# Rebuilding the sequence passes of a spectral-plus-GEGLU kernel: panels in pairs, other queues for late operands and stores, and the last down products in the passes' own banks

## The chip, the cores and the metric

The kernel runs on one core of one Trainium2 chip. The metric is the device time of one execution, in microseconds. Before the change three runs took 846.03, 844.85 and 843.11 us, median 844.85.

## The reference

The kernel computes a block with two parallel branches that are added to their input. x is 2048 tokens by 512 features, the inner size of the second branch is 1792.

```python
x = A_x
xn = _layernorm(x, axis=-1)
# branch A: Fourier mixing, DFT along the features, then along the sequence, real part
a = jnp.einsum("bsd,ed->bse", xn, dft_hid_re)
b = jnp.einsum("bsd,ed->bse", xn, dft_hid_im)
A = jnp.einsum("ts,bse->bte", dft_seq_re, a) - jnp.einsum("ts,bse->bte", dft_seq_im, b)
# branch B: GEGLU
B = jnp.einsum("bsf,fd->bsd", _gelu(xn @ w_gate) * (xn @ w_up), w_down)
return x + A + B
```

All values are float32. The sums of the sequence DFT run over 2048 tokens.

## The kernel before, in words

**Arithmetic.** A float32 product is made from three matmuls. Each operand is split into a high part, which ACT copies into the reduced type (`split_hi`, L72), and a low part, which DVE gets by subtraction (`split_lo`, L75). `mm3` (L84 to L87) adds high by high and the two crossed terms in one PSUM bank. Products of two-by-two blocks are made with seven products (numbered 0 to 6) instead of eight, on sums of blocks; what the seven products mean for the four output blocks is settled by sums before and after.

**Stages.** Up to 53 us: layernorm and the first part of the feature DFT. Then 14 units of gate and up products, in which the down products (`down`, L441) run as background items; a second part of the feature DFT; 14 more units up to 485.7 us. From there to 836.4 us run the sequence passes, with the last 14 down items among them; the change is nearly all here.

**The sequence passes.** `steps` is a list of four passes of 16 steps; a step is one block of 128 tokens that is summed over. `passes` is (0,0), (1,0), (0,1), (1,1): the column c of the output and the group g. Group 0 makes products 0, 6 and 2 (18 matmuls a step, for two row blocks j), group 1 products 5, 4, 3 and 1 (24 matmuls). A product keeps two PSUM banks through a pass. All eight banks are one pool. For a step:

- `load_step` (L639) loads the panels of the sequence DFT matrix, 128x512 each (256 KB), three for group 0 and four for group 1, on SP's queue; `sum_step` (L646) adds panels on DVE; `split_step` (L659) makes high and low parts of each.
- The other operand, the "side", comes from the scratch tensors `ab` and `sd` in DRAM. In the first pass `load_side` (L688, SP's queue) and `side_split` (L694) prepare what group 0 needs, and it stays in memory. What group 1 needs, `b` and `qr` of each token, is the late side: `load_late` (L701) issues the two loads on POOL's queue two steps ahead and `late_side` (L707) splits them; 12 tokens are done in the second pass and 4 in the third (`late_at`).
- `contract` (L777) issues the matmuls.

At the end of a pass `drain` (L738) empties the banks and `seed` (L728) fills them for the next pass, by an ACT copy of what `load_acc` (L722) has read from the scratch tensor `partial`, where the down products and the input's own terms have been added up. The drains of group 0 send adding transfers on POOL's queue (a DMA that adds to what lies in DRAM): `tot` to `partial` (L747) and `neg` to the output (L754). Those of group 1 send `v` to the output the same way (L762) and store the finished blocks with `store` (L734) on SP's queue.

**What sets the order.** The program is written out by hand, and each engine and each queue takes its instructions in the order written. The loop over `steps` (from L917) prepares panels ahead: a step's loads are issued four or fewer steps ahead (`split_upto`), its sums one step before its splits. An issue on a queue waits for the tile that it writes to be free, and what stands behind waits with it.

Of the kernel before, what the change touches and what calls it, by code (L numbers as in the profile page):

```python
# [14 lines left out]
P = 128  # L15
# [20 lines left out]
def fnet_geglu_kernel(ctx: ExitStack, tc: tile.TileContext, x, xt, cs, dh, wgu, wd, out):  # L36
# [64 lines left out]
    xnt = dram.tile([2, ND, P, CH], F32, name="xnt")  # L101

# [336 lines left out]
    D_ORDER = (0, 2, 1, 5, 4, 6, 3)  # L439
# [20 lines left out]
    def more_items(q):  # L460
        i = q % (NP // 2)
        if i == 0:
            items.extend([lambda r=r: down([q], r, range(2)) for r in D_ORDER])
        elif i % 2 == 0:
            items.extend([lambda r=r, j=j: down([q - 1, q], r, [j]) for r in D_ORDER for j in range(2)])

# [6 lines left out]
    def background(n):  # L473
# [21 lines left out]
        if n % 2 == 0 and n:  # L495
            for k in range(4):
                splits(h_split, n // 2 - 1, k)
# [24 lines left out]
    def unit(n):  # L522
# [9 lines left out]
        if n == 1:  # L532
            store_stats()
        if n in (3, 7):
            load_st((n - 3) // 4)
# [39 lines left out]
        if n == 2 * NP - 1:  # L575
            for r in SEEDED[0]:
                load_acc(0, r)
# [23 lines left out]
        if n == 2 * NP - 1:  # L601
            seed(0, SEEDED[0][0])
# [5 lines left out]
        if n == 2 * NP - 1:  # L608
            seed(0, SEEDED[0][1])
# [11 lines left out]
    SEEDED = {0: (2, 6), 1: (5, 4, 3, 1)}  # L621
    passes = [(0, 0), (1, 0), (0, 1), (1, 1)]
    steps = [(c, g, n) for c, g in passes for n in range(NS)]
    pan, pan_src, pan_hl = {}, {}, {}
# [7 lines left out]
    def split_upto(i):  # L632
        return max(i + 1, min(i + 2, 2 * NS)) if i > 2 else i + 1

    def order(i):
        c, g, n = steps[i]
        return GROUP[g] if n else SEEDED[g] + GROUP[g][:1 - g]

    def load_step(i):  # L639
        if i < len(steps):  # L640
            c, g, n = steps[i]
            for m, t in ((0, 0), (0, 1), (1, 1), (1, 0))[:3 + g]:
                pan[i, m, t] = slot("pan")
                nc.sync.dma_start(pan[i, m, t], cs[2 * c + t, m, n])

    def sum_step(i):  # L646
        if i < len(steps):
            g = steps[i][1]
            c0, c1, i1, i0 = (pan.pop((i, m, t), None) for m, t in ((0, 0), (0, 1), (1, 1), (1, 0)))
            if g == 0:  # L650
                nc.vector.tensor_add(c1, c1, i1)
                pan_src[i] = {0: c0, 6: c1, 2: i1}
            else:
                nc.vector.tensor_add(c0, c0, c1)
                nc.vector.tensor_add(c1, c0, i1)
                nc.vector.tensor_add(i1, c1, i0)
                pan_src[i] = {4: c0, 5: c1, 3: i1, 1: i0}

    def split_step(i, part=slice(None)):  # L659
        if i < len(steps):  # L660
            src = pan_src[i]
            for r in order(i)[part]:
                t = pair("ps") if i < 4 else None
                pan_hl[i, r] = (t[:, 0], t[:, 1]) if i < 4 else hl_tile("ps")
                split(pan_hl[i, r], src[r])

    av, bv, qr, w34, a0, s34, b_hl, qr_hl = ({} for _ in range(8))
# [19 lines left out]

    def load_side(n):  # L688
        if n < NS:
            av[n], w34[n] = slot("ar", F32, (P, HD)), slot("w34")  # L690
            nc.sync.dma_start(av[n], ab[n, 0, :, :HD])
            nc.sync.dma_start(w34[n], sd[n, 0])

    def side_split(n):  # L694
        if n < NS:
            t = pair("s34")
            a0[n], s34[n] = hl_half("a0"), (t[:, 0], t[:, 1])
            split(a0[n], av.pop(n))
            split(s34[n], w34.pop(n))

    def load_late(n):  # L701
        if n < NS:
            bv[n], qr[n] = slot("b"), slot("qr")
            nc.gpsimd.dma_start(bv[n], ab[n, 1])
            nc.gpsimd.dma_start(qr[n], sd[n, 1])

    def late_side(n):  # L707
        b_hl[n], t = hl_tile("bt"), pair("qrhl")
        qr_hl[n] = t[:, 0], t[:, 1]
        split(b_hl[n], bv.pop(n))  # L710
        split(qr_hl[n], qr.pop(n))
# [8 lines left out]
    acc, bank = {}, {}  # L720

    def load_acc(c, r):  # L722
        t = pair("acc", F32)
        for j in range(2):
            acc[c, r, j] = t[:, j]
            nc.gpsimd.dma_start(acc[c, r, j], partial[c, r, j])

    def seed(c, r):  # L728
        for j in range(2):
            bank[c, r, j] = ps_tile("m")  # L730
            nc.scalar.activation(bank[c, r, j], acc.pop((c, r, j)), AF.Copy)  # L731

    def store(c, h, j, src):
        nc.sync.dma_start(out[2 * h + j, 2 * c], src)  # L734

    us, vs = {}, {}

    def drain(c, r, j):  # L738
        ps = bank.pop((c, r, j))
        if r in (0, 6):  # L740
            t = ship("tot")
            if r == 0:
                nc.vector.tensor_add(t, ps, acc.pop((c, r, j)))
            else:
                nc.scalar.activation(t, ps, AF.Copy)
            for u in (5, 1) if r == 0 else (3,):
                nc.gpsimd.dma_start(partial[c, u, j], t, accum_op=OP.add)  # L747
        if r in (6, 2):
            t = ship("neg")
            if r == 6:  # L750
                nc.vector.tensor_scalar_mul(t, ps, -1.0)
            else:
                nc.scalar.activation(t, ps, AF.Copy, scale=-1.0)
            nc.gpsimd.dma_start(out[2 * int(r == 6) + j, 2 * c + 1], t, accum_op=OP.add)  # L754
        if r == 5:
            us[j] = ship("u")
            nc.scalar.activation(us[j], ps, AF.Copy)
        if r == 4:
# [4 lines left out]
        if r == 3:  # L763
            nc.vector.tensor_add(us[j], ps, us[j])
            store(c, 1, j, us[j])
        if r == 1:
# [239 lines left out]
```

## Time and profile before

| | us |
|---|---|
| median of three runs | 844.85 |
| profiled execution | 845.09 |
| its span, first to last instruction | 843.3 |
| sequence passes in it, TensorE's first to last matmul | 485.69 to 836.38 |
| TensorE busy | 808.4 |
| VectorE (DVE) busy | 690.6 |
| ScalarE (ACT) busy | 505.9 |
| GpSimd (POOL) busy | 197.6 |
| mean granted TensorE clock | 0.986 of full |

The profile is one execution taken by the hardware profiler. PE is TensorE's matmuls, PEld its weight loads, which run beside them; SP, ACT and POOL also issue DMAs, and SPq or POOLq is the waiting of a queue's issue for a semaphore. A group of instructions is named by its source line, engine and operation, `out<-in` with the program's names, the shapes, and the count; behind the bar stand its busy time, the mean of one in ns, and the idle time of the engine before it with what ended that. The chain that ended last is followed back from the last instruction: at each step to what released it. "m" are the banks of the passes, "dn" those of down products, "psh" and "psl" the high and low parts of panels.

### The profile page before, as it was taken

The page shows a single profiled execution, that of the slowest core. Times are in us where ns is not written, and L with a number is a line of the kernel's source. Part 1 is how long each engine was busy: PE and PEld are TensorE (multiplying, and loading weights), DVE is VectorE, ACT ScalarE, POOL GpSimd, SP SyncE. Part 2 cuts the span into 40 slices and gives each one's busy share as a digit, 9 for nine tenths or more (in the row PEclk, how much of TensorE's full clock was granted, in tenths as well). Part 3 has the DMA queues.
Part 4 walks back from the last instruction along what each step waited for, and adds up shares of the span by engine and source line. Part 5 has one row for each costly group of instructions (what it writes and reads, how often), then busy time and mean ns, then how long its engine had stood idle before and what let it go on. Part 6 is the DMA issues. An engine that isn't in the chain of part 4 may idle for free.

```text
span 843.3 us, 11706 instructions
## 1 busy us (share of the span) xinstructions
PE 808.4 (96%) x3514; PEld 657.0 (78%) x3514; DVE 690.6 (82%) x1288; ACT 505.9 (60%) x972; POOL 197.6 (23%) x294
## 2 busy tenths in 40 slices
PE   8999999999999999999999999998798789999996
PEld 4887878888878888888888878886586568877885
DVE  6778999888999589998898898772896699769971
ACT  5666875767777467676756867661766254465531
POOL 2410222222211333342322401233442320010001
PEclk9999999999999999999999999999799979999999
DMA  9933638787953598899789898999889976688714
GB/s 344 377 103 125 200 103 185 166 184 164 213 162 127 173 243 214 243 265 210 178 189 270 230 282 236 317 343 282 299 322 334 278 240 212 188 233 258 245 57 99
DMA packets 92543, 187.44 MB, mean 222 GB/s; under 512 B 11568, under 2 KB 14144, under 8 KB 92224
## 3 DMA queue, kind: packets, MB, share of 16 engines
q1 hardware_dynamic: 62240, 110.92, 39.5%
q0 software_dynamic: 29952, 75.52, 37.3%
q8 instruction: 27, 0.44, 0.2%
q14 instruction: 36, 0.29, 0.1%
q10 hardware_dynamic: 288, 0.26, 0.1%
HBM read 128.97 MB, written 61.87 MB: 226 GB/s over the span
## 4 chain that ended last, share of the span: by engine, by line
PE 80%; DVE 6%; DMA 5%; issue 4%; POOL 2%; ACT 2%; SPq 0%; DVEq 0%; POOLq 0%; ACTq 0%
PE m L86 30%; PE dn L86 14%; PE b L86 11%; PE a L86 8%; PE c L86 8%; PE xp L86 5%; PE sb L86 2%; DMA pan<-in_cs 2%; DMA b<-ab 2%; PE sa L86 1%; POOL partial L747 1%; DMA xraw<-xnt 1%; DVE ws L369 1%; DMA acc<-partial 1%; POOL out_y L754 1%
## 5 line engine op out<-in xcount | busy, mean ns | idle before, releaser
L72 ACT ACTIVATE psh<-pan 128x512 fp32r<-128x512 f32 x212 | 120.7, 622 | 99.5 <-PE m L86 57.3
L75 DVE TENSOR_TENSOR psl<-pan,psh 128x512 fp32r<-128x512 f32 x212 | 134.3, 684 | 17.4 <-ACT psh L72 14.0
L455 POOL DMA_DIRECT2D partial<-part x92 | 80.8, 891 | 194.1 <-ACT part L451 177.1
L86 PE MATMUL m<-psh,qrhl 128*128 128x512 f32 x256 | 86.2, 398 | 5.4 <-ACT psh L72 4.4
L451 ACT ACTIVATE part<-dn 128x512 f32<-128x512 f32 x112 | 65.8, 598 | 23.1 <-PE dn L86 21.2
L86 PE MATMUL m<-psh,s 128*128 128x512 f32 x224 | 74.3, 394 | 0.0
L86 PEld LDWEIGHTS m<-psh,qrhl 128*128 128x128 f32 x256 | 49.1, 192 | 16.4 <-ACT psh L72 4.8
L86 PE MATMUL m<-psl,qrhl 128*128 128x512 f32 x128 | 51.3, 401 | 7.1 <-DVE psl L75 7.1
L75 DVE TENSOR_TENSOR wl<-ws,wh 128x512 fp32r<-128x512 f32 x84 | 55.0, 684 | 0.0
L86 PE MATMUL m<-psh,bth 128*128 128x512 f32 x128 | 50.1, 392 | 1.3 <-ACT m L731 1.3
L72 ACT ACTIVATE wh<-ws 128x512 fp32r<-128x512 f32 x84 | 49.6, 629 | 2.1 <-PE dn L86 2.1
L86 PE MATMUL m<-psh,btl 128*128 128x512 f32 x128 | 49.8, 389 | 0.0
L86 PE MATMUL m<-psl,bth 128*128 128x512 f32 x128 | 49.8, 389 | 0.0
L86 PEld LDWEIGHTS m<-psh,s 128*128 128x128 f32 x224 | 42.8, 191 | 9.0
L86 PE MATMUL m<-psh,a 128*128 128x512 f32 x112 | 40.0, 399 | 8.1 <-ACT psh L72 8.1
L86 PE MATMUL m<-psl,s 128*128 128x512 f32 x112 | 44.1, 393 | 0.0
L762 POOL DMA_DIRECT2D out_y<-v x8 | 7.1, 1089 | 148.0 <-DVE v L82 145.0
L86 PE MATMUL b<-xT3h,w 128*128 128x512 f32 x112 | 39.2, 391 | 0.3 <-ACT w L588 0.3
L591 DVE TENSOR_TENSOR w<-c,w 128x512 f32<-128x512 f32 x28 | 19.3, 690 | 24.4 <-ACT w L588 24.3
L75 DVE TENSOR_TENSOR htl<-s,hth 128x512 fp32r<-128x512 f32 x56 | 35.9, 685 | 2.9 <-ACT hth L72 2.8
L430 DVE TENSOR_TENSOR s<-s 128x512 f32<-128x512 f32 x56 | 37.3, 687 | 0.9
L588 ACT ACTIVATE w<-b 128x512 f32<-128x512 f32 x28 | 16.7, 597 | 35.2 <-PE b L86 35.2
(290 smaller groups left out, 2282.2 us busy)
## 6 DMA issues: line engine op xcount, KB each, us to landing
pan<-in_cs SPq DMA_DIRECT2D x224, 256.0 KB, 4.7
partial<-part POOLq DMA_DIRECT2D x112, 256.0 KB, 5.2
wx<-in_wgu SPq DMA_DIRECT2D x56, 256.0 KB, 4.6
abr<-ab SPq DMA_DIRECT2D x32, 256.0 KB, 6.4
wd<-in_wd SPq DMA_DIRECT2D x28, 256.0 KB, 4.4
acc<-partial POOLq DMA_DIRECT2D x28, 256.0 KB, 5.8
d<-in_dh SPq DMA_DIRECT2D x16, 256.0 KB, 5.4
ab<-ab POOLq DMA_DIRECT2D x16, 256.0 KB, 4.4
```

The lines of the kernel that those rows point to most:

```text
L72: nc.scalar.activation(t[0], src, AF.Copy)
L75: nc.vector.tensor_sub(t[1], src, t[0].bitcast(F32))
L86: nc.tensor.matmul(ps, a[u][:, sl], b[v], start=first and r == 0, stop=last and r == 2, skip_group_check=resumed)
L369: nc.vector.tensor_tensor(r[k][:, h], u, v, op=op)
L430: nc.vector.tensor_sub(t, u, v)
L451: nc.scalar.activation(t, ps[j], AF.Copy)
L455: nc.gpsimd.dma_start(partial[sp, r, j], t, accum_op=OP.add)
L588: nc.scalar.activation(w, b, AF.Copy)
L591: nc.vector.tensor_add(w, c, w)
L747: nc.gpsimd.dma_start(partial[c, u, j], t, accum_op=OP.add)
L754: nc.gpsimd.dma_start(out[2 * int(r == 6) + j, 2 * c + 1], t, accum_op=OP.add)
L762: nc.gpsimd.dma_start(out[2 * h + j, 2 * c + 1], v, accum_op=OP.add)
```

## The change

- **Panels in pairs.** The host lays the DFT matrix out so that one transfer brings two panels, 128x1024 (L645, L646): a step is two transfers, 512 KB + 256 KB in group 0 and two of 512 KB in group 1. The splits of a pair are one ACT and one DVE instruction of 128x1024 (`split_begin`). The bytes stay.
- **Order.** The passes are now (1,0), (0,0), (1,1), (0,1), and the token order in group 1 follows the order in which late sides become ready. Late sides are loaded on SP's queue (L736, L737) two steps ahead: 12 tokens in steps 17 to 28, and the last four at steps 3, 5, 7 and 9 of the third pass and again of the fourth, so that these are made twice.
- **Fewer adding transfers.** `drain` in group 0 writes two results per row block plainly to a new scratch tensor `kept` (L797); product 2 is first subtracted from `xt` on DVE (L822). The adding transfers to the output, eight of `neg` and eight of `v`, are gone, and with them the eight copies of `xt` into the output near the start. In the group-1 passes `load_rest` (L765) reads `kept` and `xt` back, `sub_rest` and `drain_rest` (L808) subtract on DVE, and plain stores follow. The twelve adding transfers of `tot` stay (L819). All stores but the very last go to POOL's queue (L800).
- **Last down products.** For products 0, 6 and 2 the last down products are added by TensorE into the banks of the first pass (`direct`); their ACT copies and adding transfers are gone. All banks of a pass but the first pass's product 2 are now seeded.

The core of the diff:

```diff
+    kept = dram.tile([2, 2, 2, P, CH], F32, name="kept")
...
+        elif q == NP - 1:
+            for r in (0, 2, 1, 6, 5, 4, 3):
+                items.extend([lambda r=r: direct([q - 1, q], r)] if r in GROUP[0] else
+                             [lambda r=r, j=j: down([q - 1, q], r, [j]) for j in range(2)])
...
-    passes = [(0, 0), (1, 0), (0, 1), (1, 1)]
+    passes = [(1, 0), (0, 0), (1, 1), (0, 1)]
+    tokens = {0: list(range(NS)), 1: [0, 1, 2, 3, 4, 12, 5, 13, 6, 14, 7, 15, 8, 9, 10, 11]}
...
-            for m, t in ((0, 0), (0, 1), (1, 1), (1, 0))[:3 + g]:
-                pan[i, m, t] = slot("pan")
-                nc.sync.dma_start(pan[i, m, t], cs[2 * c + t, m, n])
+            a, b = pair("pan", F32), pair("pan", F32) if g else slot("pan1")
+            pan[i] = a, b
+            nc.sync.dma_start(flat(a), cs[c, n, 0])
+            nc.sync.dma_start(flat(b) if g else b, cs[c, n, 1] if g else cs[c, n, 1, :, :CH])
...
     def load_late(n):
-        if n < NS:
-            bv[n], qr[n] = slot("b"), slot("qr")
-            nc.gpsimd.dma_start(bv[n], ab[n, 1])
-            nc.gpsimd.dma_start(qr[n], sd[n, 1])
+        av[n], bv[n] = slot("qr"), slot("b")
+        nc.sync.dma_start(bv[n], ab[n, 1])
+        nc.sync.dma_start(av[n], sd[n, 1])
...
+    def load_rest(c):
+        for j in range(2):
+            rest[c, 0, j], rest[c, 1, j], rest[c, 2, j] = ship("x12"), ship("x22"), slot("kept")
+            for h, src in enumerate((kept[c, 1, j], xt[c, 1, 2 + j], kept[c, 0, j])):
+                nc.gpsimd.dma_start(rest[c, h, j], src)
...
-    def store(c, h, j, src):
-        nc.sync.dma_start(out[2 * h + j, 2 * c], src)
+    def store(c, h, t, j, src):
+        nc.gpsimd.dma_start(out[2 * h + j, 2 * c + t], src)
...
+    def drain_rest(c):
+        for j in range(2):
+            for h in range(2):
+                t = rest.pop((c, h, j))
+                nc.vector.tensor_sub(t, t, vs[j])
+                store(c, h, 1, j, t)
...
         if r in (0, 6):
             t = ship("tot")
-            if r == 0:
-                nc.vector.tensor_add(t, ps, acc.pop((c, r, j)))
-            else:
-                nc.scalar.activation(t, ps, AF.Copy)
+            nc.scalar.activation(t, ps, AF.Copy)
+            if r == 6:
+                keep(c, 0, j, t)
             for u in (5, 1) if r == 0 else (3,):
                 nc.gpsimd.dma_start(partial[c, u, j], t, accum_op=OP.add)
-        if r in (6, 2):
-            t = ship("neg")
...
-            nc.gpsimd.dma_start(out[2 * int(r == 6) + j, 2 * c + 1], t, accum_op=OP.add)
...
+        elif r == 2:
+            t = ship("x2")
+            nc.vector.tensor_sub(t, rest.pop((c, j)), ps)
+            keep(c, 1, j, t)
...
-            v = ship("v")
-            neg_sub(v, ps, us[j])
-            for h in range(2):
-                nc.gpsimd.dma_start(out[2 * h + j, 2 * c + 1], v, accum_op=OP.add)
+            vs[j] = slot("v")
+            nc.vector.tensor_add(vs[j], ps, us[j])
...
+    def direct(qs, r):
+        for j in range(2):
+            for q in qs:
+                mm3(bank[passes[0][0], r, j], wl[("d", q), r], cols(j), hl[q, r], False, False, resumed=r != 2, late=1)
...
-                nc.gpsimd.dma_start(out[2 * h + j, 2 * sp + 1], xt[sp, 1, 2 * h + j])
...
-    late_at = {NS + 2 + k: k for k in range(NS - 4)}
-    late_at.update({2 * NS + 2 * k: NS - 4 + k for k in range(4)})
+    late_at = {NS + 1 + k: n for k, n in enumerate((4, 5, 6, 7, 8, 9, 10, 11, 0, 1, 2, 3))}
+    late_at.update({p * NS + 3 + 2 * k: 12 + k for p in (2, 3) for k in range(4)})
...
-        advance(load_step, ahead + 2)
+        advance(load_step, i + 4)
...
+        if at == 0 and p == 3:
+            drain_rest(passes[2][0])
```

How the order changes on the two queues. POOL's queue at the end of the first pass, before: the ten adding transfers of the drains and the first late loads (`tot` and `neg` are the drained sums, `b` and `qr` the late side).

```order
L747 DMA partial_83<-tot_6292 128x512 x2
L747 DMA partial_83<-tot_6299 128x512 x2
L747 DMA partial_83<-tot_6322 128x512
L754 DMA out_y<-neg_6325 128x512
L747 DMA partial_83<-tot_6331 128x512
L754 DMA out_y<-neg_6334 128x512
L754 DMA out_y<-neg_6341 128x512
L754 DMA out_y<-neg_6347 128x512
L704 DMA b_6356<-ab_84 128x512
L705 DMA qr_6357<-sd_85 128x512
```

The same place after: `x2` is product 2 subtracted from `xt`, and `x12` and `old` are loads late in the second pass.

```order
L819 DMA partial_83<-tot_6190 128x512 x2
L819 DMA partial_83<-tot_6197 128x512 x2
L797 DMA kept_87<-tot_6208 128x512
L819 DMA partial_83<-tot_6208 128x512
L797 DMA kept_87<-tot_6215 128x512
L819 DMA partial_83<-tot_6215 128x512
L797 DMA kept_87<-x2_6226 128x512
L797 DMA kept_87<-x2_6232 128x512
L783 DMA x12_6711<-in_xt 128x512
L783 DMA x12_6713<-in_xt 128x512
```

Six adding transfers and four plain ones are left, and the late loads are no longer behind them. SP's queue at the same place, before: only panels, three to a step.

```order
L644 DMA pan_6350<-in_cs 128x512
L644 DMA pan_6352<-in_cs 128x512
L644 DMA pan_6354<-in_cs 128x512
L644 DMA pan_6393<-in_cs 128x512
L644 DMA pan_6395<-in_cs 128x512
L644 DMA pan_6397<-in_cs 128x512
```

SP's queue there after, from the loads that are issued in the last step of the first pass on:

```order
L646 DMA pan1_6176<-in_cs 128x512
L736 DMA b_6180<-ab_84 128x512
L737 DMA qr_6179<-sd_85 128x512
L645 DMA pan_6244<-in_cs 128x1024
L646 DMA pan1_6245<-in_cs 128x512
L736 DMA b_6249<-ab_84 128x512
L737 DMA qr_6248<-sd_85 128x512
L645 DMA pan_6279<-in_cs 128x1024
```

Each step now has a pair, a single panel and two late operands on this queue. SP's queue at the end of the third pass, before: four stores of finished blocks (`u` and `o`) stand between the panels of the next pass.

```order
L644 DMA pan_7953<-in_cs 128x512
L644 DMA pan_7955<-in_cs 128x512
L734 DMA out_y<-u_7968 128x512
L734 DMA out_y<-u_7973 128x512
L734 DMA out_y<-o_8022 128x512
L734 DMA out_y<-o_8028 128x512
L644 DMA pan_8038<-in_cs 128x512
L644 DMA pan_8040<-in_cs 128x512
```

The same place after:

```order
L645 DMA pan_7592<-in_cs 128x1024
L646 DMA pan_7593<-in_cs 128x1024
L645 DMA pan_7665<-in_cs 128x1024
L646 DMA pan_7666<-in_cs 128x1024
L645 DMA pan_7712<-in_cs 128x1024
L646 DMA pan_7713<-in_cs 128x1024
L736 DMA b_7717<-ab_84 128x512
L737 DMA qr_7716<-sd_85 128x512
```

The stores are gone from this queue; panels follow panels, and the late side of a token that is made a second time comes behind them.

More of the change, by code (lines that the diff above doesn't have):

```diff
@@ L533, in unit @@
             store_stats()
+        if n == 2 * NP - 1:
+            for r in GROUP[0]:
+                load_old(passes[0][0], r)
         if n in (3, 7):
@@ L620, in fnet_geglu_kernel @@
     GROUP = {0: (0, 6, 2), 1: (5, 4, 3, 1)}
-    SEEDED = {0: (2, 6), 1: (5, 4, 3, 1)}
-    passes = [(0, 0), (1, 0), (0, 1), (1, 1)]
-    steps = [(c, g, n) for c, g in passes for n in range(NS)]
-    pan, pan_src, pan_hl = {}, {}, {}
+    passes = [(1, 0), (0, 0), (1, 1), (0, 1)]
+    tokens = {0: list(range(NS)), 1: [0, 1, 2, 3, 4, 12, 5, 13, 6, 14, 7, 15, 8, 9, 10, 11]}
+    steps = [(c, g, n) for c, g in passes for n in tokens[g]]
+    pan, pan_hl = {}, {}
     reached = {}
@@ L630, in advance, with flat @@
         reached[f] = max(upto + 1, reached.get(f, 0))
[L632 to L637, printed above, removed]
+    def flat(t):
+        return t.rearrange("p a b -> p (a b)")
     def load_step(i):
@@ new lines, in sum_step, with prepare_step @@
+    def sum_step(i):
+        for f in sums(i):
+            f()
+    def prepare_step(i):
+        advance(sum_step, i)
+        later = sums(i + 1) if reached[sum_step] == i + 1 else []
+        reached[sum_step] = max(reached[sum_step], i + 2)
+        if reached.get(split_step, 0) <= i < len(steps):
+            reached[split_step] = i + 1
+            low = [split_begin(i, k) for k in range(2)]
+            del pan[i]
+            if len(later) < 2:
+                low[0]()
+                low.pop(0)
+        else:
+            low = []
+        for k in range(max(len(low), len(later))):
+            for f in later[k:k + 1] + low[k:k + 1]:
+                f()
@@ new lines, in split_begin, with split_step @@
+    def split_begin(i, k):
+        g = steps[i][1]
+        two = g or k == 0
+        t = (pair("ps"), pair("pl")) if two else hl_tile("ps1")
+        src = pan[i][k]
+        split_hi(t, src)
+        for h, r in enumerate((((0, 6), (2,)), ((4, 5), (3, 1)))[g][k]):
+            pan_hl[i, r] = [v[:, h] for v in t] if two else t
+        return lambda: split_lo(t, src)
+    def split_step(i):
+        if i < len(steps):
+            for k in range(2):
+                split_begin(i, k)()
+            del pan[i]
@@ L669, in load_ab @@
+    av, bv, a0, s34, b_hl, qr_hl = ({} for _ in range(6))
     def load_ab(n):
@@ L931, in fnet_geglu_kernel @@
[L931 to L942 removed]
+        chores(p, at)
@@ L943, in fnet_geglu_kernel @@
+        ahead = i + 2 if 2 < i < 2 * NS or i > 3 * NS + 4 else i + 1
+        turn = at == NS - 1 and p == 2
+        if turn:
+            split_begin(i + 1, 0)()
+            reached[split_step] = i + 2
+        elif at < NS - 1:
+            for k in range(i + 1, ahead + 1):
+                prepare_step(k)
+        if at == 0 and p == 3:
+            drain_rest(passes[2][0])
         if p == 0:
-            advance(side_split, n + 2)
+            advance(side_split, at + 2)
             while carry:
```

187 lines of the change are left out of this document (96 added, 91 removed).

## The prediction

> **What bounds the kernel now.** I read the page's busy times first, then a table by stretches, then the chain that ended last, then the waits. The first line of the page:
>
> ```profile
> PE 808.4 (96%) x3514; PEld 657.0 (78%) x3514; DVE 690.6 (82%) x1288; ACT 505.9 (60%) x972; POOL 197.6 (23%) x294
> ```
>
> TensorE is the bound over the whole span, but a share of 96% hides places where it stands still. The sequence passes are 485.7 to 836.4 us; this is the table by stretches there (columns: stretch, length, then busy time and count of PE, PEld, DVE, ACT, POOL, then granted clock, DMA share, GB/s):
>
> ```profile
> 485.00:560.00 75.00, 74.86 (x329) 61.21 (x328) 58.80 (x103) 48.55 (x96) 14.75 (x19) 1.00 0.96 289
> 560.00:600.00 40.00, 31.25 (x129) 25.05 (x128) 20.56 (x35) 17.80 (x35) 17.32 (x25) 0.89 1.05 304
> 600.00:644.00 44.00, 44.00 (x193) 36.37 (x192) 40.14 (x67) 27.66 (x51) 12.01 (x22) 0.98 0.92 328
> 644.00:680.00 36.00, 25.34 (x100) 18.75 (x99) 23.38 (x39) 18.07 (x33) 15.61 (x23) 0.90 1.00 272
> 680.00:750.00 70.00, 70.00 (x303) 57.72 (x303) 59.97 (x94) 35.72 (x64) 4.36 (x6) 0.98 0.67 202
> 750.00:765.00 15.00, 11.94 (x53) 9.57 (x52) 11.36 (x19) 6.96 (x14) 0.00 (x0) 1.00 1.04 337
> 765.00:836.00 71.00, 71.00 (x315) 58.75 (x313) 54.84 (x88) 26.62 (x48) 3.51 (x4) 1.00 0.49 145
> ```
>
> Three of seven stretches are holes. The chain that ended last (start, length, what) gives the full pace and names the holes:
>
> ```profile
> 484.96 0.69 DVE ps L75
> 485.69 1.45 PE m L86 x5
> ...
> 499.72 4.08 PE m L86 x18
> 503.80 1.36 PE dn L86 x6
> ...
> 567.59 0.88 POOL partial L747
> ...
> 585.50 0.09 POOL out_y L754
> 586.16 6.87 DMA b<-ab
> 593.12 0.64 ACT bth L72
> 596.33 45.73 PE m L86 x190
> ...
> 645.66 0.56 POOL partial L747
> ...
> 664.88 0.58 POOL out_y L754
> 665.46 7.69 DMA b<-ab
> 678.24 72.46 PE m L86 x308
> 750.70 6.54 DMA pan<-in_cs
> 760.14 76.24 PE m L86 x335
> ```
>
> A step of 18 matmuls takes 4.08 us: 0.2267 us each. The passes hold 576 (two passes of 18 by 16 steps) + 768 (two of 24 by 16) + 84 (the last down products) = 1428 matmuls, 323.7 us at that pace. They take 836.38 − 485.69 = 350.7 us (76.24 us from 760.14 end at 836.38). So **27.0 us are lost**. By the table: 40 − 129 × 0.2267 = 10.8 at the first pass end, 36 − 100 × 0.2267 = 13.3 at the second, 15 − 53 × 0.2267 = 3.0 at the third; these three make the 27.0, and what the other stretches leave over or under is within the records that are missing (about 4 matmuls).
>
> The first two holes read alike. At the pass end POOL issues ten adding transfers in a row, from 567.59 to 585.59 and from 645.66 to 665.46, and only behind them, on the same queue, stands the next late operand `b`. ACT takes its work in order, so it stands at the `b` copy with the next step's panels already in memory:
>
> ```profile
> ACT bth L72 <- DMA b<-ab: 32.1, 2, 19.8
> ...
> SPq L734 <- DVE u L764: 37.8, 4, 30.0
> ```
>
> The third hole is the last line: the stores of the outputs wait on SP's queue for their sums, and the panel loads of the next pass stand behind them; 750.70 is a panel that landed too late.
>
> **The change, part by part.** The sum is made against the profiled execution, 845.09 us with a span of 843.3; the median of the three runs, 844.85, is 0.24 lower, and a difference within 0.3% (2.5 us) is no difference that a measurement of this kernel can tell.
>
> *Late operands.* They go to SP's queue, two steps ahead of their use, so no adding transfer stands ahead of them. What they are moved past is POOL's ten transfers; what they now stand behind is panels. What comes last then at a pass end is the splits of the next step. The last bank of the old pass is freed by a DVE subtraction (0.69 us by the rows further below), ACT seeds it (0.62), and only then makes the high copy of step 17 (1.05), and DVE its low half (1.22): 3.6 us after the pass end, while the matmuls of step 16, whose panels are split by then, cover 4.08. The first two holes go: −10.8 and −13.3, which holds the cold clock too:
>
> ```profile
> 580.00:590.00 10.00, 6.78 (x30) 5.27 (x29) 0.00 (x0) 0.00 (x0) 4.29 (x6) 1.00 1.10 282
> 590.00:600.00 10.00, 4.46 (x10) 3.21 (x11) 6.22 (x11) 6.88 (x14) 6.03 (x11) 0.56 0.92 321
> ```
>
> The clock granted fell to 0.56 after the gap, so a hole costs more than its idle time; without the gap it stays at 1.00.
>
> *Adding transfers.* Ten at each group-0 end become six adding and four plain ones, and the eight of `v` become plain stores behind DVE subtractions. Nobody waits for them soon. But they take the same DMA engines as the panels, so I work out what the second pass asks of them. Rows of DMA from 560 to 600 us, then the panel row from 600 to 644:
>
> ```profile
> q0 software_dynamic: 2804, 6.76, 67.0%
> q1 hardware_dynamic: 2950, 5.35, 37.4%
> pan<-in_cs SPq DMA_DIRECT2D x19, 256.0 KB, 9.5
> ```
>
> ```profile
> pan<-in_cs SPq DMA_DIRECT2D x31, 256.0 KB, 5.3
> ```
>
> From 600 to 644, 328 GB/s filled 0.92: 357 GB/s when full, so 256 KB (0.262 MB) is 0.735 us of all engines. From 560 to 600 the software queue used 0.67 × 40 = 26.8 us for 6.76 MB; its 4.14 MB besides the ten adding ones are 11.6 us, which leaves 15.2, or 1.5 us for each adding one. The new second pass: 48 panels, 24 late operands, 4 kept, 10 early loads for the third pass = 86 × 0.735 = 63.2, and 6 × 1.5 = 9.0, together **72.2 us of DMA against 288 × 0.2267 = 65.3 us of TensorE**. Panels are asked for four steps ahead, up to 16 us, so most of the 6.9 us over is drawn from what is there already. From 600 to 644 before, TensorE ran without a hole beside ten such steps with the same operands. Bounds: 0 to +6.9. I take **+1.5**, near the lower end, since that row is the nearest.
>
> The Trainium skill (DMA: Bandwidth & Descriptors, "Issuing engines are not separate DMA queues") says that transfers of all issuing engines run on the same 16 engines and that another issuer saves only its issuing time. That speaks against the move; what it would give is rival C.
>
> *Third hole.* The stores go to POOL's queue, so panels pass: −3.0 less what is late next. DVE has, between the low halves of steps 49 and 50, four new subtractions (L808). Counting from the third pass's end, DVE does the second sum (0.69), low half, three adds, one add and the low half of step 49, and then for step 50 an add, a low half, an add, four subtractions, an add and a low half. Durations (DVE then ACT, 128x512 then 128x256):
>
> ```profile
> L75 DVE TENSOR_TENSOR psl<-pan,psh 128x512 fp32r<-128x512 f32 x212 | 134.3, 684 | 17.4 <-ACT psh L72 14.0 <-PE dn L86 1.7 <-PE m L86 0.4
> L72 ACT ACTIVATE psh<-pan 128x512 fp32r<-128x512 f32 x212 | 120.7, 622 | 99.5 <-PE m L86 57.3 <-DVE pan L655 30.7 <-DVE psl L75 3.0
> L75 DVE TENSOR_TENSOR a<-ar,a 128x256 fp32r<-128x256 f32 x14 | 5.8, 417 | 0.0
> L72 ACT ACTIVATE a<-ar 128x256 fp32r<-128x256 f32 x14 | 5.7, 407 | 2.0 <-PE m L86 2.0
> ```
>
> From these, 128x1024 is estimated at 684 + 2 × (684 − 417) = 1.22 us on DVE and 622 + 2 × (622 − 407) = 1.05 on ACT, against 1.37 and 1.24 for two single ones. Step 50's first low half then ends 11.8 us after the pass end and is needed at 10.9: **+0.5**, between 0 and 0.9, as back-to-back instructions run a little faster than their durations add.
>
> *Panels in pairs.* Same bytes, fewer instructions: 0.15 us per pair on DVE, 0.19 on ACT. Neither engine is the bound in a full stretch (40.14 of 44 us on DVE), so nothing. They cost at one place: the entry of the first pass waits for a low half (484.96 above), and step 1's is now a pair: its high copy and low half are 1.05 + 1.22 in place of 0.62 + 0.68: **+0.9** (0 to 1.5).
>
> *Down products in the banks.* 84 matmuls as before; six copies on ACT and six adding transfers fewer in a pass where TensorE has no hole (74.86 of 75): 0. The eight copies of `xt` into the output that go lie in the first 53 us on POOL, with nobody waiting: 0. The four late operands made twice, 8 ACT and 8 DVE instructions of 128x512 more in the last pass (54.84 of 71 us on DVE): 0.
>
> *Tail.* The end now:
>
> ```profile
> 833.69 0.69 DVE L764 TENSOR_TENSOR u<-m,u 128x512 f32<-128x512 f32 x1 [0.67 <-PE m L86]
> ...
> 836.81 0.42 DVE L771 COPY o<-m 128x256 f32<-128x256 f32 x1 [2.43 <-ACT o L771]
> ```
>
> DVE idled 2.43 us ahead of its last copy; four subtractions (4 × 0.69 = 2.8) now stand there, 0.3 us late, and POOL issues five plain stores behind them, the last one perhaps half a microsecond after the last copy's own: **+0.7** (0 to 2.5).
>
> **Sum:** 845.09 − 27.0 + 1.5 + 0.5 + 0.9 + 0.7 = 821.7; on the scale of the median 821.5.
>
> **The rivals.**
>
> A, the forecast, chance 0.66: 821.5, own range 816 (every added term at zero, and 2 us of entry and tail won besides) to 827.
>
> B, the second pass becomes DMA-bound, 0.18: the 6.9 us over come out in full, as the pass starts with nothing loaded ahead because adding traffic stretches landings (9.5 us against 5.3), and a gap makes a cold clock of about 2 us. For: the share of 1.05 and 72.2 against 65.3. Against: the stretch 600 to 644. 821.5 + 5.4 + 2 = 829 (the 2 as after the first hole: 0.44 of the clock missing for some 4 us from 596.33), up to 835 if it happens at both group-0 ends and the third pass starts late as well.
>
> C, the move alone wins nothing, 0.08: the late operand was late because the engines were full, not because of its place on POOL. Then each group-0 end wins only the DMA time saved, 15.2 − (9.0 + 4 × 0.735) = 3.3 us, and the third hole goes: 845.1 − 6.6 − 3.0 + 2.1 = 837.5. This is what the Trainium skill's rule above would make of it. Against: ACT and DVE at 0.00 from 580 to 590 with panels landed, and `b` issued only at 586.16.
>
> D, slower, 0.08: SP's queue holds every load now, and in the program each of its transfers waits until the eighth before it has landed. Of before, SP's own waits show this as short:
>
> ```profile
> SPq L644 <- DMA pan<-in_cs: 20.4, 33, 1.6
> ```
>  Four transfers a step in the second pass mean that landings over 2 × 4.08 = 8.2 us stretch the step. The point from which it decides: 24.4 us of saving left over 16 steps is 1.5 us a step, so landings of 2 × 5.6 = 11.2 us all through. At 12.5 (9.5 with a third more, since pairs are twice the bytes) the step is 6.25 us: 16 × 2.17 = 34.7 lost, less the 1.5 already counted: 821.5 + 33 = 855. For: 9.5 us measured in the burst with single panels. Against: 5.3 us when the burst is over, and it lasts some 15 us, not 65.
>
> That the matmuls become more or fewer is excluded: 3514 in both.
>
> **How the numbers follow.** 821.5 is A's. The range 816 to 835 holds A and B, 0.84; C and D lie outside. Faster by over 0.3% (under 842.3): A, B, C, 0.92, less 0.02 for a C that wins less; slower 0.07; the rest, 0.03, within.
>
> **What would show it.** Right: in the new profile no wait of ACT for `b` over 3 us at the first two pass ends, the clock at 1.00 through all passes, the passes' time about 326 us, no wait of SP for the last sums. Wrong: ACT waiting for `b` or DVE for a panel in the second pass, with a DMA share of 1.0 (B; D if in every step); a hole of ten us left at a pass end (C); or a stall of several us where DVE's four subtractions stand.

## The result, and the profile after

The changed kernel takes 813.85 us (median of 4 runs, 813.66 to 813.99) against 845.38 for the kernel before in the same comparison; the ratio is 0.9632, with a 95% interval of 0.9613 to 0.9650. The forecast was 821.5 with a range of 816 to 835: the direction was right, but the time lies under the range. Of the 31.2 us between the two profiled executions (845.09 and 813.86) the forecast saw 23.4.

The page's first line after:

```profile
PE 800.0 (99%) x3514; PEld 654.3 (81%) x3514; DVE 689.2 (85%) x1210; ACT 500.7 (62%) x880; POOL 178.6 (22%) x271
```

The table by stretches of the changed kernel (columns as in the prediction's table):

```profile
560.00:600.00 40.00, 40.00 (x179) 33.11 (x178) 30.21 (x42) 26.30 (x41) 7.54 (x10) 1.00 1.04 332
600.00:644.00 44.00, 44.00 (x196) 36.45 (x195) 37.98 (x52) 28.52 (x42) 12.42 (x20) 1.00 1.03 349
644.00:680.00 36.00, 36.00 (x161) 29.81 (x159) 31.90 (x41) 18.50 (x22) 8.32 (x16) 1.00 1.04 392
680.00:750.00 70.00, 69.73 (x308) 57.44 (x307) 62.52 (x80) 34.15 (x41) 7.61 (x14) 1.00 0.79 282
```

All three holes are gone. TensorE is busy throughout and its clock stays at 1.00, while the DMA engines run full (1.03 to 1.04 from 560 to 680 us) without holding it up. The chain that ended last shows it in one line, which runs from the last steps of the first pass over the whole second into the third:

```profile
546.65 97.93 PE m L86 x432
```

That is 0.2267 us a matmul, the pace of an undisturbed step. TensorE's waits from 485 us to the end of the passes, in full, before and after (us in total, times, longest):

```profile
PE m L86 <- ACT psh L72: 12.5, 2, 8.1
PE m L86 <- DVE psl L75: 7.7, 4, 3.1
PE m L86 <- ACT m L731: 2.2, 3, 0.9
```

```profile
PE m L86 <- DVE pl L75: 0.9, 2, 0.7
```

**Where the time came from.** The first matmul of the passes in the kernel before and after, from the timelines:

```profile
480.89 3.06 PE L86 MATMUL m<-ps,s 128*128 128x512 f32 x12
```

```profile
480.11 0.50 PE L86 MATMUL m<-ps,a 128*128 128x512 f32 x1
```

So the passes begin at 480.89 before the change, not at 485.69 as the table of times ahead of the prediction has it. The last matmul ends at 836.37 before and at 805.62 after. The passes took 355.5 us and now take 325.5; their 1428 matmuls at 0.2267 need 323.7. Lost were **31.8 us, now 1.8**. The passes also begin 0.8 us earlier, and what follows the last matmul fell from 6.9 to 6.5 us.

For the experiments I use this loss by stretch: length − (count − 1.7) × 0.2267, since a matmul that straddles an edge is counted on both sides (a record lasts 0.39 us, 1.7 times the pace); undisturbed stretches come out at 0 within about 0.3. The kernel before:

```profile
560.00:620.00 60.00, 51.24 (x214) 41.55 (x213) 40.56 (x68) 32.02 (x60) 21.70 (x33) 0.91 0.98 300
620.00:700.00 80.00, 69.34 (x287) 54.95 (x286) 63.24 (x102) 41.27 (x75) 24.03 (x38) 0.94 0.93 291
700.00:775.00 75.00, 71.94 (x317) 59.23 (x316) 61.47 (x96) 37.94 (x68) 3.57 (x4) 1.00 0.73 221
```

They lose 11.9, 15.3 and 3.5 us: the first, second and third pass end. The changed kernel loses nothing at the first two and 0.6 at the third.

### The profile page after: what moved, and what is told of

It reads as the page before. It is cut to its first block, busy times and chain, and to the rows that moved or that the text cites. A ratio compares the mean times of both kernels' runs of the same rounds, so it can differ in the third digit from the quotient of the medians.

```text
span 812.1 us, 11223 instructions
## 1 busy us (share of the span) xinstructions
PE 800.0 (99%) x3514; PEld 654.3 (81%) x3514; DVE 689.2 (85%) x1210; ACT 500.7 (62%) x880; POOL 178.6 (22%) x271
## 4 chain that ended last, share of the span: by engine, by line
PE 68%; issue 17%; DVE 6%; DMA 3%; ACT 3%; POOL 2%; POOLq 0%; SPq 0%; DVEq 0%; ACTq 0%
PE m L86 18%; PE dn L86 13%; PE b L86 12%; PE a L86 8%; PE c L86 8%; PE xp L86 5%; PE sb L86 2%; DMA qr<-sd 2%; PE sa L86 1%; POOL out_y L800 1%; DMA ar<-ab 1%; DVE ws L370 1%; DVE wl L75 1%; DVE s L431 1%; DVE hl L75 1%
## 5 line engine op out<-in xcount | busy, mean ns | idle before, releaser
L72 ACT ACTIVATE ps<-pan 128x1024 fp32r<-128x1024 f32 x96 | 100.5, 1059 | 93.2 <-PE m L86 48.7
L75 DVE TENSOR_TENSOR pl<-pan,ps 128x1024 fp32r<-128x1024 f32 x96 | 117.8, 1227 | 25.9 <-ACT ps L72 18.3
L86 PE MATMUL m<-ps,bth 128*128 128x512 f32 x128 | 49.8, 389 | 0.0
L86 PE MATMUL m<-pl,bth 128*128 128x512 f32 x128 | 49.8, 389 | 0.0
L86 PE MATMUL m<-ps,btl 128*128 128x512 f32 x128 | 49.8, 389 | 0.0
L86 PE MATMUL m<-ps,a 128*128 128x512 f32 x128 | 44.7, 390 | 0.0
L86 PE MATMUL m<-ps,qrh 128*128 128x512 f32 x96 | 37.3, 389 | 0.0
L86 PE MATMUL m<-pl,qrh 128*128 128x512 f32 x96 | 37.3, 389 | 0.0
L86 PE MATMUL m<-ps,qrl 128*128 128x512 f32 x96 | 37.3, 389 | 0.0
L72 ACT ACTIVATE hth<-s 128x512 fp32r<-128x512 f32 x56 | 32.4, 640 | 0.6 <-PE dn L86 0.6
```

The costliest lines, as they stand in the source:

```text
L72: nc.scalar.activation(t[0], src, AF.Copy)
L75: nc.vector.tensor_sub(t[1], src, t[0].bitcast(F32))
L86: nc.tensor.matmul(ps, a[u][:, sl], b[v], start=first and r == 0, stop=last and r == 2, skip_group_check=resumed)
```

## The experiments

Each kernel was compared with the kernel before on the same chip, whose medians there were 845.5 to 846.7 us.

**Undoing and doing the move of the late operands.** First the move alone, on the kernel before:

```diff
-            nc.gpsimd.dma_start(bv[n], ab[n, 1])
-            nc.gpsimd.dma_start(qr[n], sd[n, 1])
+            nc.sync.dma_start(bv[n], ab[n, 1])
+            nc.sync.dma_start(qr[n], sd[n, 1])
```

> The kernel before with one edit: the late operands b and qr are loaded on SP's queue, nothing else changes. Recounted, the passes before lose 31.8 us over 1428 matmuls, some 28 of them at the two group-0 ends. Theory A (place behind the ten adding transfers on POOL): both holes go almost wholly, 845 - 24 to 28 = 817 to 821. Rival C (the engines are full, the move wins nothing by itself): 840 to 846. Rival D (SP's queue is held up by late operands in each step): over 850.

Measured 830.77 us, ratio 0.9823 (0.9802 to 0.9845). No theory had it: little more than half of what theory A wanted, and far more than rival C allows. Its stretches:

```profile
570.00:625.00 55.00, 52.55 (x225) 42.93 (x225) 39.95 (x66) 32.78 (x58) 11.04 (x17) 0.97 1.07 346
625.00:690.00 65.00, 60.08 (x258) 47.56 (x257) 58.00 (x93) 35.89 (x64) 13.66 (x19) 1.00 0.99 307
690.00:765.00 75.00, 72.11 (x312) 59.21 (x311) 63.65 (x101) 38.86 (x68) 3.56 (x4) 0.98 0.72 221
```

Lost are 4.4, 6.9 and 4.7 us. The place on POOL's queue was worth 7.5 us at the first end and 8.4 at the second. 11.3 us stay at these two.

Then the order alone, with the loads still on POOL:

```diff
-        if i + 2 in late_at:
-            load_late(late_at[i + 2])
+        if i + 4 in late_at:
+            load_late(late_at[i + 4])
```

> The kernel before with one edit: the late operands stay on POOL's queue, but are issued four steps ahead in place of two, so those of the first two late steps stand ahead of the ten adding transfers. Theory A (only what stands ahead of them in the queue matters): the first hole goes, the second goes too or nearly, 817 to 823. If POOL's queue itself is the trouble (any late load on it lands late while adding transfers run), at most half is won: 830 to 845. Rival C: 840 to 846.

Measured 833.6 us, ratio 0.9851 (0.9830 to 0.9872), with 6.0 and 6.7 us lost at the two ends. That is nearly what the other queue gave: what counts most is what stands ahead, not the queue. The level that I expected was wrong as in the first run, since part of the loss has another cause.

And the move undone in the changed kernel (L736 and L737 back to `nc.gpsimd`):

> The changed kernel with one edit: the late operands go back to POOL's queue, two steps ahead as now, behind six adding and four plain transfers in place of ten adding ones. Theory A: both holes come back, smaller by the transfers that are gone: six adding ones at about 1.9 us each and four at about 1 are 15 us where ten took 19, so each hole is 4 us smaller, some 10 and 10 us: 814 + 18 to 24 = 832 to 838. If it was the fewer adding transfers that won the time: 814 to 818.

Measured 821.2 us, ratio 0.9704 (0.9686 to 0.9723). The stretches:

```profile
560.00:620.00 60.00, 55.37 (x234) 45.03 (x233) 43.45 (x60) 36.29 (x56) 22.42 (x37) 0.94 0.97 316
620.00:690.00 70.00, 70.00 (x311) 57.98 (x310) 59.11 (x77) 37.94 (x49) 22.43 (x37) 1.00 1.01 354
```

That is well under the 832 to 838 of theory A: 7.3 us come back at the first end, none at the second, probably since the next late sides are due there only at step 3 of the third pass.

**The third end.** The kernel before with its stores (L734) on `nc.gpsimd`:

> The kernel before with one edit: the stores of finished blocks go to POOL's queue. Theory: panels of the last pass no longer stand behind the stores on SP, the third hole of 3.0 to 3.4 us goes, 841.5 to 842.5. Rival: the panels land no sooner since the transfers of v add to DRAM at the same time, or the next wait is as long: 844 to 846.

Measured 841.5 us, ratio 0.9939 (0.9921 to 0.9957). As expected, and at the right place:

```profile
700.00:775.00 75.00, 75.00 (x333) 62.10 (x332) 65.04 (x102) 38.88 (x70) 5.78 (x8) 1.00 0.77 234
```

The changed kernel with its stores (L800) back on `nc.sync`:

> The changed kernel with one edit: its plain stores of finished blocks go back to SP's queue. Theory: the third hole comes back, since SP's next panels stand behind stores that wait for sums and now for subtractions too: 814 + 3 to 6 = 817 to 820. Rival (panels are loaded so far ahead now that SP's queue may stand still for a while): 813.5 to 814.5.

Measured 812.72 us, ratio 0.9604 (0.9587 to 0.9621): 1.1 us better than the change, none of the 3 to 6 us lost. The rival's reason was right, though not its level. The gain is behind the last matmul (5.5 us in place of 6.5). The same with panels loaded three steps ahead (`load_step, i + 3`):

> The changed kernel with two edits: stores of finished blocks on SP's queue, which alone made 812.7, and panels loaded three steps ahead in place of four. Theory A5 (the third hole goes by either of two things, panels asked for a step earlier or the stores off SP): it comes back, 812.7 + 2 to 4 = 815 to 817, and nothing at the group-0 ends. Rival (the third hole stays away even so, because it was the order of splits and drains): 812.5 to 813.5. If the loads of the second pass need the fourth step, the group-0 ends lose as well: over 817.

Measured 816.39 us, ratio 0.9651 (0.9632 to 0.9669), with a loss only at the third end:

```profile
690.00:760.00 70.00, 68.28 (x300) 55.84 (x299) 60.24 (x78) 34.81 (x43) 2.72 (x5) 1.00 0.71 262
```

2.4 us there, against 0.6. So the third hole is closed by either of two things: stores off SP's queue, or panels asked for one step earlier.

**What was left of the first two.** The kernel before with late operands on SP and without the line that sends `neg` to the output (`out_y<-neg`, L754):

> The kernel before with the late operands on SP's queue, and without the eight adding transfers of neg to the output, so products 6 and 2 are missing in half of the output; their ACT and DVE copies stay. Theory A2 (the 4.4 and 6.9 us that were left at the group-0 ends are DMA time): 8 adding transfers at 1.5 us are gone, and both rests go but for 2 us or so: 831 - 7 to 11 = 820 to 824. Rival (hand-over of banks): the rest at the second end stays, 827 to 831.

Measured 825.17 us, ratio 0.9755 (0.9734 to 0.9776), between the two.

```profile
570.00:625.00 55.00, 55.00 (x244) 45.53 (x244) 45.30 (x75) 34.88 (x63) 8.08 (x13) 1.00 1.06 365
625.00:690.00 65.00, 61.07 (x265) 49.05 (x264) 59.80 (x96) 35.74 (x65) 9.72 (x14) 1.00 0.90 280
```

The first end's 4.4 us are gone but for 0.1, and panels issued from 560 to 600 us land in 6.7 us in place of 9.6: it was DMA time of adding transfers. At the second end 5.3 stay. There DVE comes late. Its timeline in this run, without a gap between the two rows:

```profile
629.90 2.49 DVE L75 TENSOR_TENSOR psl<-pan,psh 128x512 fp32r<-128x512 f32 x4
632.30 1.28 DVE L743 TENSOR_TENSOR tot<-m,acc 128x512 f32<-128x512 f32 x2
```

and ACT's beside it:

```profile
633.02 1.20 ACT L731 ACTIVATE m<-acc 128x512 f32<-128x512 f32 x2 [5.17 <-DVE tot L743]
```

The drain `tot` stands behind four low halves of the coming step, and the seed of the next pass waits 5.2 us for it. The last matmul of product 0 ends at 628.92, so the drain begins 3.4 us late.

The changed kernel with sums and splits of a coming step ahead of the drains (`elif at < NS - 1:` made `else:`):

> The changed kernel with one edit: at the two group-0 ends the sums and splits of the coming step stand ahead of the drains on ACT and DVE, as in the kernel before, in place of behind them. Theory A4 (the 5.3 us left at the second end when late operands had moved and adding transfers were fewer are the hand-over of banks: drains and seeds wait behind splits): 2 to 5 us come back, nearly all at the second end, 816 to 819. Rival (the 5.3 us were panels that landed late): 813.5 to 814.5.

Measured 814.46 us, ratio 0.9631 (0.9616 to 0.9647), nothing lost at either end. In the changed kernel as it is, this order costs nothing; as I put it, the theory fell.

The expectation calls it the order of the kernel before, and that it is not. The four low halves ahead of `tot` are those of step 32 (steps count from 0), the first of the third pass, and the changed kernel too makes them ahead of its drains. The edit moves the step after it, 33, and at the first end step 17. In the kernel before, step 33 stands behind the drains, and at the first end step 17 stands between them. The next two rows of DVE's timeline, in the run without `neg`'s transfers, show it for step 33:

```profile
634.77 1.29 DVE L751 TENSOR_SCALAR neg<-m 128x512 f32<-128x512 f32 x2 [1.18 <-ACT tot L745]
639.28 2.50 DVE L75 TENSOR_TENSOR psl<-pan,psh 128x512 fp32r<-128x512 f32 x4 [3.22 <-ACT psh L72]
```

What differs at this place is the drain itself. In the changed kernel ACT alone drains products 0 and 6 (L815), where DVE took part in both before (L743, L751), so the seeds that follow these two no longer wait for DVE. At DVE's only drain there, product 2, DVE has been waiting for TensorE:

```profile
630.33 1.37 DVE L822 TENSOR_TENSOR x<-x,m 128x512 f32<-128x512 f32 x2 [2.97 <-PE m L86]
```

No run undoes this part alone.

The changed kernel with ten adding transfers again:

```diff
             for u in (5, 1) if r == 0 else (3,):
                 nc.gpsimd.dma_start(partial[c, u, j], t, accum_op=OP.add)
+            nc.gpsimd.dma_start(partial[c, r, j], t, accum_op=OP.add)
```

> The changed kernel with four adding transfers more at each group-0 end (each drained sum of products 0 and 6 is also added to a part of the scratch tensor that nobody reads any more), so ten adding and four plain ones, with the late operands on SP. Theory A2 (what the late operands' move alone left of the holes, 4.4 us at the first and 6.9 at the second pass end, is DMA time of adding transfers): 4 more of 1.5 us each, 6 us of DMA per pass end on engines that are full there: 3 to 8 us come back, 817 to 822. Rival (what was left was the hand-over of banks by DVE and ACT, which the change rewrote): 814 to 815.

Measured 817.34 us, ratio 0.9662 (0.9637 to 0.9688), 1.7 us lost at each end, at the low end of what was expected. DVE's wait for panels from 560 to 640 us in the changed kernel, in this run, and in the kernel before with late operands on SP:

```profile
DVE pan L653 <- DMA pan<-in_cs: 3.3, 3, 1.9
```

```profile
DVE pan L653 <- DMA pan<-in_cs: 10.2, 4, 4.4
```

```profile
DVE pan L651 <- DMA pan<-in_cs: 16.2, 8, 4.1
```

With more adding transfers DVE waits longer for panels, and so comes later to the end of the second pass. From here on the parts were undone with ten adding transfers in place, where no time is to spare. Splits by halves:

```diff
-        split_hi(t, src)
+        parts = [([v[:, h] for v in t], src[:, h]) for h in range(2)] if two else [(t, src)]
+        for u, s in parts:
+            split_hi(u, s)
...
-        return lambda: split_lo(t, src)
+        return lambda: [split_lo(u, s) for u, s in parts]
```

> The changed kernel with ten adding and four plain transfers at each group-0 end (which alone made 817.3) and with the splits of panel pairs made by halves, 128x512 at a time on ACT and DVE, as in the kernel before; loads stay in pairs. Theory A6 (DVE was late at the second end because of all its work of the second pass: 0.15 us a pair less is slack): 2 to 4 us more than 817.3 at the group-0 ends, 819 to 821. Rival (DVE's time does not matter, only when panels land): 816.5 to 818.

Measured 816.83 us, ratio 0.9651 (0.9624 to 0.9677): the pairs' saving on DVE is worth nothing here. The profile has the loss as 3.3 and 0.4 us, not 1.7 and 1.7, so how a loss divides between the two ends is less sure than its sum.

Six adding transfers more late in the first pass:

```diff
+        if p == 0 and n in (12, 13, 14):
+            for j in range(2):
+                nc.gpsimd.dma_start(partial[c, GROUP[0][n - 12], j], extra, accum_op=OP.add)
```

> The changed kernel with ten adding and four plain transfers at each group-0 end and with six adding transfers more in the first pass, two each at its steps 12, 13 and 14 (of zeros, to a part of the scratch tensor that nobody reads any more), in place of the six that the down products' banks took away. Theory A7 (the adding transfers of the down products late in the first pass are part of the DMA debt with which the second pass starts): 2 to 6 us more than 817.3, at both group-0 ends, 819 to 823. Rival: 816.5 to 818.

Measured 819.94 us, ratio 0.9689 (0.9663 to 0.9716): 2.6 us more, above each of the four runs with ten adding transfers alone (816.52 to 819.37). The loss is 5.5 us at the first end and 0.2 at the second. Late sides a step later (`NS + 1 + k` made `NS + 2 + k`):

> The changed kernel with ten adding and four plain transfers at each group-0 end, and the late sides of the second pass one step later (steps 18 to 29), as in the kernel before. Theory: one step later brings the last late sides nearer to the second end, where DVE has to hand over banks: 1 to 3 us more than 817.3, at the second end. Rival (a step later relieves the first end, where the adding transfers run): 815.5 to 817.

Measured 818.81 us, ratio 0.9675 (0.9648 to 0.9701), 1.9 and 3.3 us lost. The place is as expected, 1.6 more at the second end, but the 1.5 us lie within the spread of the runs that they are compared with. All three:

> The three of this call together on the kernel with ten adding and four plain transfers at each group-0 end: splits by halves, six adding transfers more late in the first pass, late sides a step later. The kernel before with late operands on SP lost 11.3 us at the group-0 ends, the kernel with ten adding ones alone 3.4. If the three are what lies between: 817.3 + 5 to 9 = 822 to 826. If something else of the change holds the rest: below 820.

Measured 819.54 us, ratio 0.9685 (0.9653 to 0.9718): 3.0 and 2.6 us lost, not enough. Then the preparations ahead of the drains once more, on this kernel and on the one with ten adding transfers alone:

> The run with ten adding transfers and the three other parts undone (819.5, 5.7 us lost at the group-0 ends), and the sums and splits of the coming step put ahead of the drains, as in the kernel before. Alone, with DVE having time to spare, that order cost nothing; here panels land late and DVE comes late to the pass end. Theory A8 (the order costs only when panels are late, and then makes up the rest of the kernel before's 11.3 us): 3 to 6 us more, 822 to 826. Rival (the order never matters): 819 to 820.5.

> The changed kernel with ten adding and four plain transfers at each group-0 end (817.3, 3.4 us lost at the ends) and the sums and splits of the coming step ahead of the drains. By A8 here too it costs, since panels land late: 1 to 4 us more, 818.5 to 821. Rival: 816.5 to 818.

Measured 824.7 us, ratio 0.9739 (0.9711 to 0.9768), and 819.53, ratio 0.9677 (0.9649 to 0.9704): 5.2 and 2.2 us more, both at the level that A8 had. The first of the two by stretches:

```profile
545.00:605.00 60.00, 57.72 (x251) 46.49 (x250) 38.91 (x65) 35.05 (x63) 17.10 (x21) 1.00 1.06 310
605.00:690.00 85.00, 79.23 (x341) 65.07 (x340) 73.81 (x122) 50.34 (x92) 24.21 (x38) 0.96 1.03 355
```

3.5 and 8.1 us lost, 11.6 together, where the kernel before with late operands on SP loses 11.3. The sums agree, but the waits do not. At the second end TensorE waits here once, for a seed that stands behind the high copies of step 33:

```profile
PE m L86 <- ACT m L778: 5.8, 1, 5.8
```

In the kernel before with late operands on SP it waits for three seeds that came late by DVE's drains, and later for a low half:

```profile
639.57 0.50 PE L86 MATMUL m<-psh,qrhl 128*128 128x512 f32 x1 [1.62 <-ACT m L731]
642.05 0.50 PE L86 MATMUL m<-psh,bth 128*128 128x512 f32 x1 [0.82 <-ACT m L731]
644.14 0.50 PE L86 MATMUL m<-psh,bth 128*128 128x512 f32 x1 [0.44 <-ACT m L731]
653.65 0.50 PE L86 MATMUL m<-psl,qrhl 128*128 128x512 f32 x1 [1.99 <-DVE psl L75]
```

So these runs show that one order can cost nothing in the changed kernel and 5 us where panels land late. They do not show that it made the rest of the kernel before, which does not have it.

**Two more.** Each pair loaded by two transfers of 256 KB into the same tile:

```diff
-            nc.sync.dma_start(flat(a), cs[c, n, 0])
+            for t in range(2):
+                nc.sync.dma_start(a[:, t], cs[c, n, 0, :, t * CH:(t + 1) * CH])
```

(and `b` likewise)

> The changed kernel with each panel pair loaded by two transfers of 256 KB (2 KB a row) in place of one of 512 KB (4 KB a row), into the same tile; splits stay in pairs. Theory (same bytes, same DMA time): 814 to 815. Rival A3 (the longer rows are what lets the second pass keep up: 72 us of DMA against 65 of TensorE by the rates of the kernel before): DMA falls behind in the second pass, 3 to 11 us lost, 817 to 825.

Measured 814.12 us, the median of 813.92, 813.94, 814.30 and one execution of 2090.7 that nothing explains; ratio 0.9619 (0.9599 to 0.9640). That is no difference, so the larger transfers win nothing by themselves.

Only step 1's pair split by halves (`halves = i == 1 and two`):

> The changed kernel with one edit: the panel pair of step 1 is split by halves, 128x512 at a time, as before the change. Theory: TensorE idles 0.66 us for the low half of step 1's pair at the entry of the first pass; by halves this wait is 0 to 0.2 us: 0.4 to 0.8 us less, 813.1 to 813.5. Rival (the wait is for the loads or for ACT's other work, not for the pair): 813.7 to 814.0.

Measured 813.27 us, ratio 0.9615 (0.9601 to 0.9630): 0.6 us less than the change. TensorE's second product of step 1, in the changed kernel and in this run:

```profile
485.38 0.50 PE L86 MATMUL m<-pl,a 128*128 128x512 f32 x1 [0.66 <-DVE pl L75]
```

```profile
484.93 0.50 PE L86 MATMUL m<-pl,a 128*128 128x512 f32 x1
```

With the stores on SP as well:

> The changed kernel with both edits that looked better alone: stores of finished blocks on SP's queue, and the panel pair of step 1 split by halves. If the gains are at different places (tail and entry) they add: 812.7 less 0.4 to 0.8 = 811.9 to 812.3. If the entry gains nothing: 812.7.

Measured 812.10 us, ratio 0.9601 (0.9585 to 0.9617): the two gains, at the entry and behind the last matmul, add. This is the best version found, 1.75 us under the change.

## Why the prediction was wrong, step by step

The forecast's terms against the two profiled executions: it had −24.1 us for the passes (−27.0 and +1.5, +0.5, +0.9), the trace −30.0; +0.7 for the tail, the trace −0.45; nothing ahead of the passes, the trace −0.8.

- **"So 27.0 us are lost" was the step that failed.** It set 1428 matmuls against the time from 485.69 us, but the passes begin at 480.89: step 0 and the first matmul of step 1, 19 matmuls or 4.3 us, had been done by then, and 0.5 us were lost ahead of it. The loss was 31.8. The check by stretches agreed only because it had errors of its own: counts with straddling matmuls are some 0.4 us too high a stretch, and what was missing from 600 to 644 and from 680 to 750 (clock 0.98 in both) was put down to missing records. That alone is 4.8 of the 7.8 us that the forecast was short.
- **"The first two holes go", for the late operands' sake: right in the sum, wrong in the reason.** The move alone gave 15.9 us. That both holes went whole was luck, as far as this reason goes: other parts of the change took away the rest. Rival C fell, and so did the claim that the place on the queue was the whole. Of the 27.2 us lost at the two ends the place was 15.9 (7.5 and 8.4). 5.9 more went with four adding transfers at each end (4.3 and 1.6, from the run without `neg`). The last 5.4 us, nearly all at the second end, are by the trace a DVE that comes late and a seed that waits for its drain. That ACT makes these drains in the changed kernel is the likely reason why they are gone; this is argued, not shown.
- **"Adding transfers: nobody waits for them soon" was wrong in effect.** Their price of 1.5 us of all DMA engines was about right (the time of POOL's queue rises by some 10 us with eight more of them, 1.3 each, and falls by some 14 without the eight of `neg`, 1.7 each), but beside late operands on SP they make panels late, and late panels a late DVE. The forecast had this as a cost of the change that it might still pay (rival B) and not as a cost of the kernel before that the change takes away. The down products' six adding transfers, put at 0, belong here: six like them cost 2.6 us where no time was to spare.
- **The second pass at +1.5 us cost 0.** The DMA engines are full from 560 to 680 us, as worked out, but move more than was assumed: 23.5 MB from 565 to 630 us, in 65 us where the forecast had 72.2, and 392 GB/s from 644 to 680, not 357. Rivals B and D did not come about. (The saving left in rival D, 24.4 us, is 23.4 by the forecast's own sum; nothing hangs on it.)
- **The third hole at −3.0 + 0.5 was near:** 3.5 lost before, 0.6 now. The stores' move, to which I gave it, does it in the kernel before, but was not needed: with panels asked for a step earlier the stores are better left on SP.
- **The entry at +0.9 was right:** 0.66 us idle and a short slow clock; splitting by halves gave 0.8 us of the passes' time back. Panels in pairs were worth nothing elsewhere, as forecast. The estimates for 128x1024 held, 1.22 and 1.05 us:

```profile
L75 DVE TENSOR_TENSOR pl<-pan,ps 128x1024 fp32r<-128x1024 f32 x96 | 117.8, 1227 | 25.9 <-ACT ps L72 18.3 <-PE m L86 4.9 <-ACT bth L72 2.5
L72 ACT ACTIVATE ps<-pan 128x1024 fp32r<-128x1024 f32 x96 | 100.5, 1059 | 93.2 <-PE m L86 48.7 <-DVE pan L655 16.1 <-DVE pan L656 10.6
```

- **The tail at +0.7 was −0.45.** DVE's four subtractions were over in time: its last copy begins 0.44 us after the last matmul, as before. And the last transfers land sooner, 2.4 and 3.1 us in place of 5.2 and 4.9, probably since no adding transfer runs beside them; the five stores on POOL that I feared take part of it back, as the run with stores on SP shows.

```profile
806.06 0.42 DVE L837 COPY o<-m 128x256 f32<-128x256 f32 x1
```

The last two transfers before and after:

```profile
out_y<-o ACTq DMA_DIRECT2D x1, 128.0 KB, 5.2
out_y<-o SPq DMA_DIRECT2D x1, 128.0 KB, 4.9
```

```profile
out_y<-o ACTq DMA_DIRECT2D x1, 128.0 KB, 2.4
out_y<-o SPq DMA_DIRECT2D x1, 128.0 KB, 3.1
```

- **The 0.8 us ahead of the passes** I had not forecast. 0.3 of it is a wait of TensorE for ACT at 462.98 us that is gone; the rest is not explained, and the passes' start differs by as much between kernels with the same code ahead of it (480.77 to 481.51 us).

What stays open is the last 5.4 us. The run with four edits loses nearly as much at the two ends as the kernel before with late operands on SP (11.6 and 11.3 us), but one of its edits makes an order that neither kernel has, and the waits differ. The run that would decide it, the changed kernel with ten adding transfers and DVE in the drains of products 0 and 6 again, was not made.

## What to carry to other kernels

Take a loss as the length of a stage less its work, with the stage's first and last instruction looked up in the timeline; a count and a start that come from different views don't belong together. When a stall has one visible cause, ask what would be late next with it gone, here panels and then DVE at the pass end, and look for the parts of the change that remove just that. The price of an edit depends on the time that is left to spare: one order of preparations cost nothing in the changed kernel, 2.2 us with more adding transfers and 5.2 with three more parts undone. When you undo a part, make sure from the source and the trace that the kernel before had what you put back. A queue's order is a resource: a load behind ten slow transfers waits for all of them.

## What was not expected of the hardware

While adding transfers ran, the DMA engines were full (share 1.10 from 580 to 590 us before) but moved 282 GB/s; nearly without them they moved 392 at a share of 1.04 (644 to 680 us of the changed kernel, where the last one had been issued at 642.69). Transfers of 512 KB with rows of 4 KB and of 256 KB with rows of 2 KB gave the same time (813.85 and 814.12 us).
